# Pinning the opening of a fused attention and two-layer kernel, a score bank pair for each of its first four units, and weight words scaled on ACT from the sixth half on

## The chip, the core and the metric

The kernel runs as one program on one core of a Trainium2 chip. The metric is the device time of one execution in microseconds (us). The engines go by the profile's names: PE (TensorE, matmuls; PEld are its weight loads), DVE (VectorE), ACT (ScalarE), POOL (GpSimd, hardly used) and SP (SyncE, which issues nearly all DMAs). Each takes its own instructions strictly in the order in which the built program holds them and waits for others through semaphores.

## What is computed

The reference is local plus global attention, followed by two dense layers, all in float32:

```python
a_l = sm(s_l)                                   # window of 32 each way + 32 global keys
out_l = np.matmul(a_l, np.concatenate([v_g, v_l], axis=2))
out_g = np.matmul(sm(s_g), v_all)
x = concat([out_g, out_l]).transpose(0, 2, 1, 3).reshape(2176, 512)
h = x @ w_in;  g = np.maximum(h, 0.0) + alpha * np.minimum(h, 0.0);  x = g @ w_out      # first layer
h = x @ w_in2; g = h * np.clip(h + 3.0, 0.0, 6.0) / 6.0;             out = g @ w_out2   # second layer
```

There are 4 batches, 8 heads of 64, 512 local and 32 global positions; each layer goes 512 to 2048 to 512.

## The kernel before

**Attention.** The local attention is cut into 32 units (batch, half of the sequence, pair of heads), `local_units`, L177. A unit is 16 score matmuls into two PSUM banks (`s_ps`, L208), four row reductions with the mask on DVE (`p`, L226), four exponentials with their sums on ACT (L230), sums and reciprocals on DVE (`st`, `rs`, L232 and L234), four PE transposes (`pt_ps`, L241) and their copy to SBUF (`pt`, ACT, L243), 16 matmuls with the values (`o_ps`, L254) and a scaling on DVE (`xo`, L260). Units go in pairs that share the two score banks. Four units (0 to 3, the heads of the first 256 rows) make the first half of the first block of the first layer.

**Inputs of the first layer.** The `xo` tiles are transposed on PE (`xt_ps`, L426) and split into a high and a low float32r part: the high one by ACT (`xt`, L409), the low one by DVE (L410).

**Weights.** They arrive as 64-bit words, 512 columns (one *half*: one of 16 columns j of w_in or of w_out) per DMA (`raw`, L95). A half takes on ACT one scaling of the low words (`raw`, L110), then the scaling of the high words (`z`) on DVE (L113) or, from half `SCALED_ON_DVE` on, on ACT (L116), two DVE steps on bits (`z`, L121 and L123), a high part by ACT (`wt`, L132) and a low part by DVE (`wt`, L133). `z` has two buffers and `raw` five. From the half before `SCALED_ON_DVE` on, L169 begins the next half, too, before this one ends. The order of halves is in_0, in_1, out_0, in_2, out_1, in_3 and so on (L143); halves count from 0.

**First layer.** Block 0 goes in 20 steps. In the first four, `h_tile` (L453) makes 12 matmuls of 256 columns (`h_ps`, L459), one column j after the other, then `act` (L464) the PReLU: ACT `t` (L469), DVE `t` (L471), ACT `g` (L477), DVE `g` (L478). Two steps later the products with w_out follow (`y_ps`, L490). Four steps on, the second 256 rows (units 4 to 7) join. Between them attention steps and conversions are recorded (L1002 to L1008).

**What sets the order.** A scheduler places the recorded instructions by its own estimate of times; only what is wrapped in `here` (L100) stays at its place in the program. Before the first tile the conversions stand at attention steps 3, 4 and 5 (`CONVERT`, L44), and one more at step 0 of block 0 (L1002, L1003).

Of the kernel before, what the change touches and what calls it, by code (L numbers as in the profile page):

```python
# [21 lines left out]
HP = H // 2  # L22
# [20 lines left out]
SCALED_ON_DVE = 8  # L43
CONVERT = (3, 4, 5)  # L44
# [12 lines left out]
def fused_kernel(ctx, tc, qkE, vE, qgz, kN, vN, vgN, w1, w2, consts, out):  # L57
# [42 lines left out]
    here = tc.keep_in_program_order  # L100

# [17 lines left out]
    def end_float32(z, low, high):  # L119
        bits = z.bitcast(U32)  # L120
        nc.vector.scalar_tensor_tensor(out=bits, in0=bits, scalar=3, in1=low, op0=ALU.logical_shift_left,  # L121
                                       op1=ALU.bitwise_or)
        nc.vector.scalar_tensor_tensor(out=bits, in0=high, scalar=0x80000000, in1=bits, op0=ALU.bitwise_and,  # L123
                                       op1=ALU.bitwise_or)
        return z
# [4 lines left out]
    def split_w(begun, wt, m):  # L130
        z = end_float32(*begun)
        nc.scalar.copy(wt[:, m, 0, :], z)  # L132
        nc.vector.tensor_tensor(out=wt[:, m, 1, :], in0=z, in1=wt[:, m, 0, :].bitcast(F32), op=ALU.subtract)  # L133

    class Weights:
# [21 lines left out]

        def convert(self, halves):
            for _ in range(halves):
                k = self.next  # L160
                if k == 2 * NJ:
                    return
                self.fetch(EARLY)
                j, m = self.seq[k]
                if j not in self.wt:
                    self.wt[j] = wp.tile([128, 2, 2, 512], F32R, tag="w", name="wt", bufs=NJ)
                self.begin(k)
                if k + 1 >= SCALED_ON_DVE:
                    self.begin(k + 1)  # L169
                split_w(self.begun.pop(k), self.wt[j], m)  # L170
                self.fetch(k + EARLY + 1)
                self.next += 1
# [4 lines left out]
    def local_units(att):  # L177
        units = [(b, hf, hp) for b in range(B) for hf in range(2) for hp in range(HP)]
        q_t, k_t, v_t, p_t, rs_t, pt_t, v2 = {}, {}, {}, {}, {}, {}, {}
# [16 lines left out]
        def scores(*us):  # L196
            s = [bank("s0_ps"), bank("s1_ps")]
            for e, u in enumerate(us):
                b, hf, hp = units[u]
                q, k = q_t.pop(u), k_t.pop(u)  # L200
                for i in range(2):
                    for g in range(4):
                        at = 128 * i + W * g
                        o = W * (start_of(8 * hf + 4 * i + g) - 12 * hf)
                        to = 256 * e + 128 * i
                        for h in range(2):
                            rows = slice(64 * h, 64 * h + 64)
                            nc.tensor.matmul(s[h][W * g:W * g + W, to:to + 128], lhsT=q[rows, at:at + W],  # L208
                                             rhs=k[rows, o:o + 128], start=True, stop=True)
            for e, u in enumerate(us):  # L210
                softmax(u, [x[:, 256 * e:256 * e + 256] for x in s])

        def softmax(u, s):
# [8 lines left out]
            for i in range(2):  # L222
                m = 1 if (hf, i) == (0, 0) else 2 if (hf, i) == (1, 1) else 0
                for h in range(2):
                    n = 2 * i + h
                    nc.vector.tensor_tensor_reduce(  # L226
                        out=p[:, n, :], in0=s[h][:, 128 * i:128 * i + 128], in1=mask_sb[:, m, :],
                        op0=ALU.add, op1=ALU.min, scale=-0.125, scalar=-NEG, accum_out=st[:, 1, n:n + 1])
            for n in range(4):
                nc.scalar.activation(p[:, n, :], p[:, n, :], AF.Exp, bias=st[:, 1, n:n + 1], scale=-1.0,  # L230
                                     accum_out=st[:, 2, n:n + 1])
            nc.vector.tensor_scalar(out=st[:, 3, :], in0=st[:, 2, :], scalar1=1e-9, scalar2=None, op0=ALU.add)  # L232
            rs_t[u] = att.tile([128, 4], F32, tag="rs", name="rs", bufs=FIRST_UNITS)
            nc.vector.reciprocal(out=rs_t[u], in_=st[:, 3, :])  # L234
            p_t[u] = p

        def transposes(u):
            p = p_t.pop(u)
            t = bank("pt_ps")
            for n in range(4):  # L240
                nc.tensor.transpose(t[:, 128 * n:128 * n + 128], p[:, n, :], ident_sb)  # L241
            pt_t[u] = att.tile([128, 4, 128], F32, tag="pt", name="pt", bufs=2)
            nc.scalar.copy(pt_t[u], t.rearrange("p (n q) -> p n q", n=4))  # L243

        def values(*us):
            o = bank("o_ps")
            for e, u in enumerate(us):
                pt, v = pt_t.pop(u), v_t.pop(u)
                for i in range(2):
                    for h in range(2):  # L250
                        n = 2 * i + h
                        to = 256 * e + D * n
                        for g in range(4):
                            nc.tensor.matmul(o[W * g:W * g + W, to:to + D],  # L254
                                             lhsT=pt[:, n, W * g:W * g + W], rhs=v[:, 4 * i + g, h, :],
                                             start=True, stop=True)
            for e, u in enumerate(us):
                b, hf, hp = units[u]
                x = outs.tile([128, 2, 128], F32, tag="xo", name="xo", bufs=8)
                nc.vector.tensor_tensor(out=x.rearrange("p i (h d) -> p (i h) d", h=2),  # L260
                                        in0=o[:, 256 * e:256 * e + 256].rearrange("p (n d) -> p n d", n=4),
                                        in1=rs_t.pop(u)[:, :, None].to_broadcast([128, 4, D]), op=ALU.mult)
                xo[b, hf, hp] = x

# [13 lines left out]
        yield  # L278
        pairs = [(u, u + 1) for u in range(0, n, 2)]
        scores(*pairs[0])  # L280
        yield
        scores(*pairs[1])
        here(nc.vector.tensor_scalar(out=c1_sb, in0=alpha_sb, scalar1=-1.0, scalar2=1.0, op0=ALU.mult, op1=ALU.add))
        load(4)
# [8 lines left out]
        for u in pairs[1]:  # L293
            transposes(u)
        yield
        values(*pairs[1])
        yield
        for j in range(2, len(pairs) + 1):
            if j > 2:
                for u in pairs[j - 1]:  # L300
                    transposes(u)
# [3 lines left out]
            if j < len(pairs):  # L305
                scores(*pairs[j])
# [100 lines left out]

    def split_x(src, dst, n):
        nc.scalar.copy(dst[:, 0, :n], src)  # L409
        nc.vector.tensor_tensor(out=dst[:, 1, :n], in0=src, in1=dst[:, 0, :n].bitcast(F32), op=ALU.subtract)  # L410
# [4 lines left out]
    def x_transposed(pieces, each=1):  # L415
# [3 lines left out]
        for hp in range(HP):  # L419
# [3 lines left out]
            for piece in pieces:  # L423
                x = xo.pop(("g", hp) if piece == "g" else (*piece, hp))
                for i in range(1 if piece == "g" else 2):
                    nc.tensor.transpose(t[:, at:at + 128], x if piece == "g" else x[:, i, :], ident_sb)  # L426
# [26 lines left out]
    def h_tile(xt, wts, parts):  # L453
        ps = bank("h_ps")
        for a, b, j, at in parts:
            k = 0
            for c in range(NC):
                for wl, xl in ((0, 0), (1, 0), (0, 1)):
                    nc.tensor.matmul(ps[:, a:b], lhsT=wts[j][:, 0, wl, 128 * c:128 * c + 128],  # L459
                                     rhs=xt[c][:, xl, at:at + b - a], start=k == 0, stop=k == 3 * NC - 1)  # L460
# [3 lines left out]
    def act(layer, ps, parts):  # L464
# [3 lines left out]
        if layer == 0:  # L468
            nc.scalar.activation(t[:, a:b], ps[:, a:b], AF.Relu, scale=-1.0)  # L469
            for c, d, j, _ in parts:  # L470
                nc.vector.scalar_tensor_tensor(out=t[:, c:d], in0=t[:, c:d], scalar=c1_sb[:, j:j + 1],  # L471
                                               in1=ps[:, c:d], op0=ALU.mult, op1=ALU.add)
        else:
            nc.scalar.activation(t[:, a:b], ps[:, a:b], AF.Relu, bias=half_sb, scale=1.0 / 6.0)
            nc.vector.scalar_tensor_tensor(out=t[:, a:b], in0=t[:, a:b], scalar=1.0, in1=ps[:, a:b],
                                           op0=ALU.min, op1=ALU.mult)
        nc.scalar.copy(g[:, 0, a:b], t[:, a:b])  # L477
        nc.vector.tensor_tensor(out=g[:, 1, a:b], in0=t[:, a:b], in1=g[:, 0, a:b].bitcast(F32), op=ALU.subtract)  # L478
        return g

    def y_tiles(layer, y, g, wts, parts, lanes=False):
        for a, b, j, at in parts:
# [3 lines left out]
            for (wl, gl), c in steps:  # L486
                first = a == 0 and j == 0 and (wl, gl) == (0, 0)
                last = j == NJ - 1 and (wl, gl) == (0, 1) and (not lanes or b == 512)
                if layer == 0:
                    nc.tensor.matmul(y[c][:, at:at + b - a], lhsT=wts[j][:, 1, wl, 128 * c:128 * c + 128],  # L490
                                     rhs=g[:, gl, a:b], start=first, stop=last, skip_group_check=lanes)
                else:
                    nc.tensor.matmul(y[c], lhsT=g[:, gl, 128 * c:128 * c + 128], rhs=wts[j][:, 1, wl, :],
                                     start=first, stop=last)
# [485 lines left out]
    k = 0  # L980
    while not ready(blocks[0][:1]):
        attention_steps(1)
        k += 1
        if k in CONVERT:
            W1.convert(1)
    xt = x_tiles()
    x_split(x_transposed(blocks[0][:1]), xt, 0)
    spare["y"] = False
    for bi in range(len(blocks)):
# [5 lines left out]
        for s in range(end + LAG):  # L995
            if s < end:
                if bi == 0:
# [23 lines left out]
            if s >= LAG:  # L1021
                y_tiles(0, y, gs.pop(s - LAG), W1.wt, active(bi, s - LAG), bi == 0)
# [84 lines left out]
```

## Time and profile before

| what | us |
|---|---|
| median of three runs | 825.03 (823.32, 825.47, 825.03) |
| the profiled execution | 823.27 |
| its span, first to last instruction | 821.5 |
| PE busy | 809.2 (99%) |
| DVE busy | 596.6 (73%) |
| ACT busy | 423.3 (52%) |
| mean granted share of PE's clock | 0.993 |

The span is one execution of the program on the core; what lies outside of it, 1.8 us, is start and end. Shares are means over stages with different limits, so the opening has to be read by stretches.

### The profile page before, as it was taken

What the parts mean: (1) busy time and instruction counts of PE and PEld (TensorE: products, weight loads), DVE (VectorE), ACT (ScalarE), POOL (GpSimd) and SP (SyncE); (2) the same over time, 40 slices, a digit from 0 to 9 for tenths busy, and PEclk for the clock granted to TensorE, in tenths of its full rate; (3) what the DMA queues carried; (4) which work ended last, traced back from release to release, by engine and by line L of the source; (5) the groups of instructions that cost most, each with busy time, mean ns of one, the idle gap of its engine ahead of it and who ended that gap; (6) DMA issues with size and microseconds to landing.
All of it is one profiled execution on the core that took longest, in us unless ns stands there. A gap on an engine that the chain in (4) does not pass through costs nothing.

```text
span 821.5 us, 17564 instructions
## 1 busy us (share of the span) xinstructions
PE 809.2 (99%) x6980; PEld 714.1 (87%) x6980; DVE 596.6 (73%) x1247; ACT 423.3 (52%) x886; POOL 0.2 (0%) x4
## 2 busy tenths in 40 slices
PE   7999999999999999999999999999999999999997
PEld 4788888888888887888999988889999888899997
DVE  4998997477888776756878847778867576678443
ACT  5887996445656664544545524434553343333431
POOL 0000000000000000000000000000000000000000
PEclk8899999999999999999999999999999999999999
DMA  9985674347879767788495575576686656655663
GB/s 334 354 276 193 244 251 149 107 175 261 280 252 305 246 236 250 276 282 284 159 335 174 167 257 180 183 225 207 185 268 212 201 186 204 180 181 159 208 182 108
DMA packets 78002, 183.09 MB, mean 223 GB/s; under 512 B 6752, under 2 KB 28512, under 8 KB 77920
## 3 DMA queue, kind: packets, MB, share of 16 engines
q1 hardware_dynamic: 77728, 181.83, 66.9%
q8 instruction: 55, 0.90, 0.4%
q14 instruction: 27, 0.22, 0.1%
q10 hardware_dynamic: 192, 0.13, 0.1%
HBM read 139.47 MB, written 42.47 MB: 221 GB/s over the span
## 4 chain that ended last, share of the span: by engine, by line
PE 93%; DVE 2%; ACT 2%; DMA 1%; SPq 1%; issue 0%; DVEq 0%; ACTq 0%
PE y_ps L490 23%; PE h_ps L459 22%; PE o_ps L904 20%; PE k_ps L816 19%; PE s_ps L208 2%; PE o_ps L254 2%; PE yr_ps L789 1%; PE hr_ps L768 1%; DMA raw<-in_w 1%; PE pt_ps L241 1%; ACT p L230 1%; PE go_ps L391 1%; PE xt_ps L426 1%; PE gs_ps L346 1%; DVE z L121 1%
## 5 line engine op out<-in xcount | busy, mean ns | idle before, releaser
L490 PE MATMUL y_ps<-g,wt 128*128 128x512 f32 (+2 forms) x1008 | 205.4, 353 | 0.2 <-ACT g L477 0.2
L459 PE MATMUL h_ps<-xt,wt 128*128 128x512 f32 (+2 forms) x1008 | 203.2, 352 | 1.9 <-DVE xt L410 1.6
L459 PEld LDWEIGHTS h_ps<-xt,wt 128*128 128x128 f32 x1008 | 169.2, 190 | 24.0 <-DVE xt L410 2.0
L490 PEld LDWEIGHTS y_ps<-g,wt 128*128 128x128 f32 x1008 | 166.7, 189 | 22.2 <-issue 0.8
L904 PE MATMUL o_ps<-ws,gh 128*128 128x256 f32 x896 | 160.9, 283 | 0.1
L816 PE MATMUL k_ps<-bt,ws 128*128 128x512 f32 x672 | 157.2, 390 | 0.0
L816 PEld LDWEIGHTS k_ps<-bt,ws 128*128 128x128 f32 x672 | 124.6, 188 | 24.9
L904 PEld LDWEIGHTS o_ps<-ws,gh 128*128 128x128 f32 x896 | 138.8, 192 | 0.6 <-issue 0.3
L904 PE MATMUL o_ps<-ws,gl 128*128 128x256 f32 x448 | 124.2, 283 | 0.0
L830 DVE TENSOR_TENSOR gl<-far,gh 128x1024 fp32r<-128x1024 f32 x56 | 68.5, 1223 | 42.3 <-ACT gh L829 42.3
L829 ACT CAST gh<-far 128x1024 fp32r<-128x1024 f32 x56 | 58.7, 1048 | 74.4 <-PE o_ps L904 70.6
L904 PEld LDWEIGHTS o_ps<-ws,gl 128*128 128x128 f32 x448 | 84.9, 192 | 0.0
L471 DVE SCALAR_TENSOR_TENSOR t<-t,c_sb,h_ps 128x512 f32<-128x512 f32 (+2 forms) x84 | 53.0, 641 | 30.0 <-ACT t L469 29.6
L750 ACT ACTIVATE t<-far,half_sb 128x512 f32<-128x512 f32 x48 | 34.8, 724 | 77.1 <-DVE far L746 77.1
L469 ACT ACTIVATE t<-h_ps 128x512 f32<-128x512 f32 (+2 forms) x76 | 41.5, 550 | 51.0 <-PE h_ps L459 49.0
L478 DVE TENSOR_TENSOR g<-t,g 128x512 fp32r<-128x512 f32 (+2 forms) x76 | 48.0, 632 | 20.8 <-ACT g L477 18.4
L477 ACT CAST g<-t 128x512 fp32r<-128x512 f32 (+2 forms) x76 | 43.8, 576 | 34.7 <-DVE t L471 33.4
L230 ACT ACTIVATE p<-p,st 128x128 f32<-128x128 f32 x128 | 49.7, 389 | 11.6 <-DVE st L226 11.6
L121 DVE SCALAR_TENSOR_TENSOR z<-z,raw 128x512 uint32<-128x512 uint32 x64 | 43.6, 689 | 9.1 <-ACT z L116 4.6
L110 ACT ACTIVATE raw<-raw,quarter_sb 128x512 uint32<-128x512 uint32 x64 | 49.3, 772 | 1.6 <-DMA raw<-in_w 1.6
L123 DVE SCALAR_TENSOR_TENSOR z<-raw,z 128x512 uint32<-128x512 uint32 x64 | 43.4, 688 | 0.6
L751 DVE SCALAR_TENSOR_TENSOR far<-t,far 128x512 f32<-128x512 f32 x48 | 33.1, 689 | 11.8 <-ACT t L750 11.8
(102 smaller groups left out, 786.5 us busy)
## 6 DMA issues: line engine op xcount, KB each, us to landing
raw<-in_w SPq DMA_DIRECT2D x64, 512.0 KB, 5.4
ws<-wo SPq DMA_DIRECT2D x60, 512.0 KB, 3.8
ws<-wi SPq DMA_DIRECT2D x56, 512.0 KB, 4.4
v_t<-in_vE SPq DMA_DIRECT2D x32, 512.0 KB, 6.9
qk_t<-in_qkE SPq DMA_DIRECT2D x32, 368.0 KB, 5.1
wi<-raw SPq DMA_DIRECT2D x16, 512.0 KB, 3.3
wi<-parts SPq DMA_DIRECT2D x16, 512.0 KB, 4.5
wo<-raw SPq DMA_DIRECT2D x16, 512.0 KB, 2.9
```

The lines of the kernel that those rows point to most:

```text
L110: here(nc.scalar.activation(low, low, AF.Relu, bias=quarter_sb, scale=0.9 * 2.0 ** -29))
L121: nc.vector.scalar_tensor_tensor(out=bits, in0=bits, scalar=3, in1=low, op0=ALU.logical_shift_left, op1=ALU.bitwise_or)
L230: nc.scalar.activation(p[:, n, :], p[:, n, :], AF.Exp, bias=st[:, 1, n:n + 1], scale=-1.0, accum_out=st[:, 2, n:n + 1])
L459: nc.tensor.matmul(ps[:, a:b], lhsT=wts[j][:, 0, wl, 128 * c:128 * c + 128], rhs=xt[c][:, xl, at:at + b - a], start=k == 0, stop=k == 3 * ...
L471: nc.vector.scalar_tensor_tensor(out=t[:, c:d], in0=t[:, c:d], scalar=c1_sb[:, j:j + 1], in1=ps[:, c:d], op0=ALU.mult, op1=ALU.add)
L477: nc.scalar.copy(g[:, 0, a:b], t[:, a:b])
L478: nc.vector.tensor_tensor(out=g[:, 1, a:b], in0=t[:, a:b], in1=g[:, 0, a:b].bitcast(F32), op=ALU.subtract)
L490: nc.tensor.matmul(y[c][:, at:at + b - a], lhsT=wts[j][:, 1, wl, 128 * c:128 * c + 128], rhs=g[:, gl, a:b], start=first, stop=last, skip_g ...
L816: nc.tensor.matmul(bank, lhsT=wt[:, wl, 128 * c:128 * c + 128], rhs=bt[x][:, c, xl, 0:w], start=first and k == 0, stop=k == 5, skip_group_ ...
L829: nc.scalar.copy(hi, src)
L830: nc.vector.tensor_tensor(out=lo, in0=src, in1=hi.bitcast(F32), op=ALU.subtract)
L904: mm = nc.tensor.matmul(bank, lhsT=part[:, jp, 128 * c:128 * c + 128], rhs=wo[:, jp, 256 * wl:256 * wl + 256], start=opens, stop=k == NP / ...
```

## The change

`SCALED_ON_DVE` goes from 8 to 5, so the high words of halves 5, 6 and 7 are scaled by ACT, and the beginning of the next half is recorded ahead from half 4 on. A function `keep` pins everything up to the first PReLU step into program order. Units 0 to 3 are recorded one by one, each with two score banks of its own. The copies of the transposed probabilities of units 0, 1 and 2 go from ACT to DVE. The first half's conversion and the beginning of the second are woven between the transposes of x; no other conversion stands ahead of the first tile, and step 0 records none ahead of it (`if s`). The two DMAs of the values of units 4 and 5 come ahead of that of half 3.

```diff
-SCALED_ON_DVE = 8
-CONVERT = (3, 4, 5)
+SCALED_ON_DVE = 5
...
     here = tc.keep_in_program_order
+    pinned = {"on": True}
+
+    def keep(x):
+        return here(x) if pinned["on"] else x
...
+        for u in range(FIRST_UNITS):
+            s = [bank("s0_ps"), bank("s1_ps")]
+            scores(u, s, 0)
+            maxima(u, s, 0)
+            exponentials(u)
+        t = {}
+        for u in range(2):
+            t[u] = transposes(u)
+            sums(u)
+            transposed(u, t[u], nc.vector.tensor_copy)
+        keep(nc.vector.tensor_scalar(out=c1_sb, in0=alpha_sb, scalar1=-1.0, scalar2=1.0, op0=ALU.mult, op1=ALU.add))
+        t[2] = transposes(2)
+        values(0)
+        sums(2)
+        transposed(2, t[2], nc.vector.tensor_copy)
+        t[3] = transposes(3)
+        sums(3)
+        values(1)
+        yield
         load(5)
-        yield
-        for u in pairs[0]:
-            transposes(u)
-        yield
-        values(*pairs[0])
+        transposed(3, t[3], nc.scalar.copy)
+        yield
         load_v(4)
         load_v(5)
...
-    k = 0
-    while not ready(blocks[0][:1]):
-        attention_steps(1)
-        k += 1
-        if k in CONVERT:
-            W1.convert(1)
     xt = x_tiles()
-    x_split(x_transposed(blocks[0][:1]), xt, 0)
+    half = W1.one()
...
+    attention_steps(1)
+    t0 = turn(0)
+    high_x(t0, xt[0], 256)
+    attention_steps(1)
+    t1 = turn(1)
+    high_x(t1, xt[1], 256)
+    next(half)
+    low_x(t0, xt[0], 256)
+    low_x(t1, xt[1], 256)
+    next(half)
+    attention_steps(1)
+    next(half)
+    t2 = turn(2)
...
+    for _ in half:
+        pass
+    half = W1.one()
+    next(half)
+    next(half)
...
-                    W1.convert(W1.needed(converted(s)) - W1.next)
-                    W1.convert(min(1, W1.needed(converted(s) + AHEAD) - W1.next))
+                    if s:
+                        W1.convert(W1.needed(converted(s)) - W1.next)
+                    if s:
+                        W1.convert(min(1, W1.needed(converted(s) + AHEAD) - W1.next))
                 parts = active(bi, s)
-                gs[s] = act(0, h_tile(xt, W1.wt, parts), parts)
+                gs[s] = act(h_tile(xt, W1.wt, parts), parts, half)
+                pinned["on"] = False
```

`next(half)` runs a conversion up to its next `yield`: first its beginning (L110, L113 of before), then the bit steps, then the two parts. The rest of the diff splits helpers so that they can be recorded apart, and drops a branch that nothing calls.

**ACT around the first tiles.** `wt` is a half's high part, `raw` the scaling of low words, `p` an exponential, `xt` the high part of x, `t` and `g` the PReLU. Before, from the first `wt` (half 0) on:

```order
L132 CAST wt<-z 128x512
L409 CAST xt<-xt_ps 128x256
L132 CAST wt<-z 128x512
L110 ACTIVATE raw<-raw,quarter_sb 128x512
L409 CAST xt<-xt_ps 128x256
L110 ACTIVATE raw<-raw,quarter_sb 128x512
L132 CAST wt<-z 128x512 x2
L230 ACTIVATE p,st<-p,st 128x128 x3
```

In the changed kernel, from the third `wt` (half 2) to the fourth (half 3):

```order
L136 CAST wt<-z 128x512
L113 ACTIVATE raw<-raw,quarter_sb 128x512
L242 ACTIVATE p,st<-p,st 128x128
L515 ACTIVATE t<-h_ps 128x256
L242 ACTIVATE p,st<-p,st 128x128 x5
L113 ACTIVATE raw<-raw,quarter_sb 128x512 x2
L521 CAST g<-t 128x256
L113 ACTIVATE raw<-raw,quarter_sb 128x512
L269 COPY pt<-pt_ps 128x512
L136 CAST wt<-z 128x512
```

Before, half 3 follows half 2 at once and both stand ahead of all exponentials of the second four units; now six exponentials, three scalings of low words and three other rows stand between the two.

**PE around the third tile.** `h_ps` x12 is one column of the first layer, `pt_ps` and `s_ps` belong to units 4 to 7. Before, from the rest of the second column on:

```order
L459 MATMUL h_ps<-xt,wt 128x256 x13
L241 MATMUL pt_ps<-consts_sb,p 128x128 x5
L459 MATMUL h_ps<-xt,wt 128x256 x12
L241 MATMUL pt_ps<-consts_sb,p 128x128 x3
L490 MATMUL y_ps<-g,wt 128x256 x8
```

In the changed kernel, from the second column on:

```order
L505 MATMUL h_ps<-xt,wt 128x256 x12
L264 MATMUL pt_ps<-consts_sb,p 128x128 x2
L534 MATMUL y_ps<-g,wt 128x256 x4
L264 MATMUL pt_ps<-consts_sb,p 128x128
L534 MATMUL y_ps<-g,wt 128x256 x8
L264 MATMUL pt_ps<-consts_sb,p 128x128 x5
L505 MATMUL h_ps<-xt,wt 128x256
L216 MATMUL s_ps<-qk_t 32x128 x17
L505 MATMUL h_ps<-xt,wt 128x256 x11
```

The third column (the one that needs half 3) has moved behind the first 12 products with w_out, and the scores of units 6 and 7 stand behind its first matmul. From the 24 `h_ps` of the third and fourth column of the second 256 rows on, PE's rows run alike in both programs.

## Rows read from the trace of the kernel before

**Rows 1.** Busy time of each engine by stretches (us of the span).
```profile
core 0: us, PE busy (x) PEld busy (x) DVE busy (x) ACT busy (x) POOL busy (x), PEclk, DMA share, GB/s
...
30.00:40.00 10.00, 9.13 (x180) 7.24 (x183) 9.40 (x36) 9.43 (x28) 0.00 (x0) 1.00 0.89 300
40.00:50.00 10.00, 8.29 (x164) 6.93 (x156) 9.42 (x39) 9.61 (x34) 0.00 (x0) 1.00 0.90 310
60.00:800.00 740.00, 740.00 (x6033) 656.33 (x6015) 542.59 (x1062) 373.66 (x741) 0.00 (x0) 1.00 0.67 218
```

**Rows 2.** Chain that ended last, about 50 us: start, length, what.
```profile
49.50 0.34 DVE xt L410
49.89 1.57 PE h_ps L459 x11
```

**Rows 3.** Timeline of PE: start, length, line, count, [idle before, releaser].
```profile
16.97 1.08 PE L254 MATMUL o_ps<-v_t,pt 128*32 128x64 f32 x32
...
23.22 2.45 PE L459 MATMUL h_ps<-xt,wt 128*128 128x256 f32 x10
...
29.02 1.69 PE L459 MATMUL h_ps<-xt,wt 128*128 128x256 f32 x12
...
54.56 3.04 PE L459 MATMUL h_ps<-xt,wt 128*128 128x256 f32 x24
```

**Rows 4.** Timeline of ACT, 6 to 49 us.
```profile
6.65 0.40 ACT L230 ACTIVATE p<-p,st 128x128 f32<-128x128 f32 x1 [4.64 <-DVE st L226]
...
29.50 0.39 ACT L230 ACTIVATE p<-p,st 128x128 f32<-128x128 f32 x1
...
29.89 0.77 ACT L110 ACTIVATE raw<-raw,quarter_sb 128x512 uint32<-128x512 uint32 x1
30.55 0.36 ACT L469 ACTIVATE t<-h_ps 128x256 f32<-128x256 f32 x1
30.81 0.39 ACT L477 CAST g<-t 128x256 fp32r<-128x256 f32 x1
31.11 1.05 ACT L243 COPY pt<-pt_ps 128x512 f32<-128x512 f32 x2
...
43.53 1.14 ACT L132 CAST wt<-z 128x512 fp32r<-128x512 f32 x2
...
48.11 0.67 ACT L116 ACTIVATE z<-raw 128x512 f32<-128x512 f32 x1
```

**Rows 5.** Timeline of DVE, 13 to 49 us.
```profile
14.26 0.42 DVE L113 TENSOR_SCALAR z<-raw 128x512 f32<-128x512 f32 x1
...
24.27 0.68 DVE L121 SCALAR_TENSOR_TENSOR z<-z,raw 128x512 uint32<-128x512 uint32 x1
24.99 0.69 DVE L123 SCALAR_TENSOR_TENSOR z<-raw,z 128x512 uint32<-128x512 uint32 x1
25.60 0.68 DVE L133 TENSOR_TENSOR wt<-z,wt 128x512 fp32r<-128x512 f32 x1
26.20 0.28 DVE L226 CUSTOM_DVE_ANT_0 p<-s_ps,consts_sb 128x128 f32<-128x128 f32 x1
...
27.68 0.69 DVE L133 TENSOR_TENSOR wt<-z,wt 128x512 fp32r<-128x512 f32 x1
...
38.29 0.74 DVE L260 TENSOR_TENSOR xo<-o_ps,rs 128x256 f32<-128x256 f32 x2
...
48.29 0.39 DVE L410 TENSOR_TENSOR xt<-xt_ps,xt 128x256 fp32r<-128x256 f32 x1
```

**Rows 6.** The one DVE copy out of a PSUM bank, all its runs.
```profile
L1039 DVE COPY ev<-y_ps x10: 425/681/692, 141.8 to 479.7; 128x512 f32<-128x512 f32 x6, 128x256 f32<-128x256 f32 x2, 128x384 f32<-128x384 f32 x2
```

**Rows 7.** The same stretches view for PE with the granted clock.
```profile
4.99:15.23 10.24, 7.64 (x220) 1.00 1.00 358
15.23:25.47 10.24, 8.55 (x135) 0.50 1.03 407
25.47:35.71 10.24, 9.76 (x189) 1.00 0.94 356
```

More of the change, by code (lines that the diff above doesn't have):

```diff
@@ L120, in end_float32 @@
         bits = z.bitcast(U32)
[L121 to L124, printed above, removed]
+        keep(nc.vector.scalar_tensor_tensor(out=bits, in0=bits, scalar=3, in1=low, op0=ALU.logical_shift_left,
+                                            op1=ALU.bitwise_or))
+        keep(nc.vector.scalar_tensor_tensor(out=bits, in0=high, scalar=0x80000000, in1=bits, op0=ALU.bitwise_and,
+                                            op1=ALU.bitwise_or))
         return z
@@ L131, in split_w @@
         z = end_float32(*begun)
-        nc.scalar.copy(wt[:, m, 0, :], z)
-        nc.vector.tensor_tensor(out=wt[:, m, 1, :], in0=z, in1=wt[:, m, 0, :].bitcast(F32), op=ALU.subtract)
+        yield
+        keep(nc.scalar.copy(wt[:, m, 0, :], z))
+        keep(nc.vector.tensor_tensor(out=wt[:, m, 1, :], in0=z, in1=wt[:, m, 0, :].bitcast(F32), op=ALU.subtract))
+        yield
     class Weights:
@@ L156, in begin, with one @@
                 self.begun[k] = begin_float32(self.raw.pop(k), k < SCALED_ON_DVE)
+        def one(self):
+            k = self.next
+            self.fetch(EARLY)
+            j, m = self.seq[k]
+            if j not in self.wt:
+                self.wt[j] = wp.tile([128, 2, 2, 512], F32R, tag="w", name="wt", bufs=NJ)
+            self.begin(k)
+            yield
+            if k + 1 >= SCALED_ON_DVE:
+                self.begin(k + 1)
+            yield from split_w(self.begun.pop(k), self.wt[j], m)
+            self.fetch(k + EARLY + 1)
+            self.next += 1
         def convert(self, halves):
             for _ in range(halves):
-                k = self.next
-                if k == 2 * NJ:
+                if self.next == 2 * NJ:
                     return
[L163 to L172, printed above, removed]
+                for _ in self.one():
+                    pass
     xo = {}
@@ L194, in load_v, with scores, maxima @@
             nc.sync.dma_start(out=v_t[u], in_=vE[b, hp, :, 8 * hf:8 * hf + 8])
[L196 to L213, printed above, removed]
+        def scores(u, s, to):
+            b, hf, hp = units[u]
+            q, k = q_t.pop(u), k_t.pop(u)
+            for i in range(2):
+                for g in range(4):
+                    at = 128 * i + W * g
+                    o = W * (start_of(8 * hf + 4 * i + g) - 12 * hf)
+                    for h in range(2):
+                        rows = slice(64 * h, 64 * h + 64)
+                        mm = nc.tensor.matmul(s[h][W * g:W * g + W, to + 128 * i:to + 128 * i + 128],
+                                              lhsT=q[rows, at:at + W], rhs=k[rows, o:o + 128], start=True, stop=True)
+                        if u < FIRST_UNITS or u == FIRST_UNITS and i == g == h == 0:
+                            here(mm)
+        def maxima(u, s, to):
             b, hf, hp = units[u]
@@ L278, in local_units @@
         yield
+        load(4)
         pairs = [(u, u + 1) for u in range(0, n, 2)]
-        scores(*pairs[0])
+        for u in range(FIRST_UNITS):
+            s = [bank("s0_ps"), bank("s1_ps")]
+            scores(u, s, 0)
+            maxima(u, s, 0)
+            exponentials(u)
+        t = {}
+        for u in range(2):
+            t[u] = transposes(u)
+            sums(u)
+            transposed(u, t[u], nc.vector.tensor_copy)
[7 more added lines that the diff above has]
+        values(1)
         yield
-        scores(*pairs[1])
-        here(nc.vector.tensor_scalar(out=c1_sb, in0=alpha_sb, scalar1=-1.0, scalar2=1.0, op0=ALU.mult, op1=ALU.add))
-        load(4)
         load(5)
+        transposed(3, t[3], nc.scalar.copy)
         yield
-        for u in pairs[0]:
-            transposes(u)
-        yield
-        values(*pairs[0])
         load_v(4)
         load_v(5)
-        for u in pairs[1]:
-            transposes(u)
+        values(2)
         yield
-        values(*pairs[1])
+        values(3)
         yield
@@ L406, in fused_kernel, with high_x, low_x, x_transposed @@
     rows = out.rearrange("(b s) d -> b s d", s=S)
+    def high_x(src, dst, n):
+        keep(nc.scalar.copy(dst[:, 0, :n], src))
+    def low_x(src, dst, n):
+        keep(nc.vector.tensor_tensor(out=dst[:, 1, :n], in0=src, in1=dst[:, 0, :n].bitcast(F32), op=ALU.subtract))
     def split_x(src, dst, n):
-        nc.scalar.copy(dst[:, 0, :n], src)
-        nc.vector.tensor_tensor(out=dst[:, 1, :n], in0=src, in1=dst[:, 0, :n].bitcast(F32), op=ALU.subtract)
+        high_x(src, dst, n)
+        low_x(src, dst, n)
     def x_tiles():
         return [work.tile([128, 2, 512], F32R, tag="xt", name="xt", bufs=HP) for _ in range(HP)]
-    def x_transposed(pieces, each=1):
+    def x_transposed(pieces, each=1, pairs=range(HP)):
         n = sum(128 if x == "g" else 256 for x in pieces)
         parts = []
-        for hp in range(HP):
+        for hp in pairs:
             if hp % each == 0:
@@ L458, in h_tile, with act @@
                 for wl, xl in ((0, 0), (1, 0), (0, 1)):
-                    nc.tensor.matmul(ps[:, a:b], lhsT=wts[j][:, 0, wl, 128 * c:128 * c + 128],
-                                     rhs=xt[c][:, xl, at:at + b - a], start=k == 0, stop=k == 3 * NC - 1)
+                    mm = nc.tensor.matmul(ps[:, a:b], lhsT=wts[j][:, 0, wl, 128 * c:128 * c + 128],
+                                          rhs=xt[c][:, xl, at:at + b - a], start=k == 0, stop=k == 3 * NC - 1)
+                    keep(mm)
                     k += 1
         return ps
-    def act(layer, ps, parts):
+    def act(ps, parts, between=()):
         t = work.tile([128, 512], F32, tag="t", name="t", bufs=TB)
@@ L467, in act, with y_tiles @@
         a, b = parts[0][0], parts[-1][1]
[L468 to L478, printed above, removed]
+        keep(nc.scalar.activation(t[:, a:b], ps[:, a:b], AF.Relu, scale=-1.0))
+        for c, d, j, _ in parts:
+            keep(nc.vector.scalar_tensor_tensor(out=t[:, c:d], in0=t[:, c:d], scalar=c1_sb[:, j:j + 1],
+                                                in1=ps[:, c:d], op0=ALU.mult, op1=ALU.add))
+        for _ in between:
+            pass
+        keep(nc.scalar.copy(g[:, 0, a:b], t[:, a:b]))
+        keep(nc.vector.tensor_tensor(out=g[:, 1, a:b], in0=t[:, a:b], in1=g[:, 0, a:b].bitcast(F32),
+                                     op=ALU.subtract))
         return g
-    def y_tiles(layer, y, g, wts, parts, lanes=False):
+    def y_tiles(y, g, wts, parts, lanes=False):
         for a, b, j, at in parts:
@@ L488, in y_tiles @@
                 last = j == NJ - 1 and (wl, gl) == (0, 1) and (not lanes or b == 512)
[L489 to L494, printed above, removed]
+                nc.tensor.matmul(y[c][:, at:at + b - a], lhsT=wts[j][:, 1, wl, 128 * c:128 * c + 128],
+                                 rhs=g[:, gl, a:b], start=first, stop=last, skip_group_check=lanes)
     half_sb = const.tile([128, 1], F32, name="half_sb")
```

64 lines of the change are left out of this document (43 added, 21 removed).

## The prediction

> **What bounds the kernel now.** I read the stretches first: from 60 to 800 us PE is busy for 740.00 of 740 us, while DVE and ACT have a fifth to a half of it free [rows 1]. Nothing that DVE or ACT gain or lose there shows. From 30 to 50 it is the other way round: DVE is busy for 9.40 and 9.42 of ten, ACT for 9.43 and 9.61, and PE has holes [rows 1]. The chain of waits says when the roles change: its last DVE piece, the low part of x, begins at 49.50, and from 49.89 it is PE alone [rows 2]. So I need one number: how far the change moves the moment at which PE reaches its solid part. As a mark I take the 24 `h_ps` matmuls at 54.56 [rows 3]. From there PE's rows are the same in both orders, and ahead of it stand the same 72 `h_ps` and 48 `y_ps` matmuls; whatever moves the mark moves the end by as much.
>
> **What it adds, removes and moves.**
>
> *Scaling of halves 5, 6 and 7.* DVE loses 3 x 0.34 (the step from 14.26 to 14.60) [rows 5] = 1.0 us, ACT gains 3 x 0.67 [rows 4] = 2.0 us. Neither is covered: both engines are full until 50.
>
> *Copies of `pt`.* ACT loses 3 x 0.52 [rows 4]. DVE has not made this copy; its copy of the same size out of a bank took 0.68 at the median [rows 6], so I take steps of 0.60, with ACT's 0.52 and 0.80 as bounds. They come at 10 to 13 us.
>
> *DMAs.* The values of units 4 and 5 pass the words of half 3. At the 0.4 MB per us of the full queue (407 GB/s in 15 to 25 us) [rows 7], two transfers of 0.52 MB make these 2.6 us later. I put their landing at 24 to 25; DVE asks for half 3 at 28. They cost nothing; with that cover gone, up to 2.6.
>
> *Conversions.* This is the large edit. Before, half 3 stood ahead of the exponentials of the second four units, and its low part began on DVE at 27.68 [rows 5]; the third column of the first layer, which needs it, started at 29.02 [rows 3]. Now it stands behind six exponentials and three scalings for later halves. I work the queues forward in their new order, each step as long as its row, each wait for what the program waits for. The same working of the order before puts the third column at 29.0 and the mark at 54.3 (trace 29.02 and 54.56).
>
> 1. *To the first tile.* One unit's scores now suffice for the first exponential, which I put at 5.65 instead of 6.65 [rows 4]. Sixteen in a row at 0.39 end at 11.9. Transposes, the values of unit 1 and two transposes of x take until 13.0 (an estimate from the same rows). ACT: two `xt` and a `pt` copy, then the low words of half 0 (0.66), to 14.8. DVE: `z` 0.72, `z` 0.61 [rows 5], `xo` 0.4, to 16.6. PE at the lower clock: two transposes, then 16 value matmuls in 1.08 [rows 3], to 18.3; `xo` and two more transposes: **19.2**. Before, only one matmul ran ahead of 23.22 [rows 3]. So the front is indeed earlier.
> 2. *To half 2.* 12 matmuls at 0.245 (2.45 for ten) [rows 3] end at 22.2, with their latency 22.4. ACT `t` and `wt` of half 1, then on DVE `wt` 0.60, `g` 0.39, scaling 0.34, `z` 0.60, two maxima 0.42, `z` 0.69 [rows 5]: the high part of half 2 starts on ACT at **26.4**.
> 3. *ACT to half 3.* `wt` 0.57, then `raw` 0.66, `p` 0.39, `t` 0.26, five `p` 1.95, two `raw` 1.32, `g` 0.30, `raw` 0.66, `pt` 0.52 [rows 4]. That is 6.6, so 33.0; with `wt` itself, DVE's low part and with it the third column start at **33.6**. DVE had half 3's bits ready near 30.4. Against 27.68 and 29.02 this is +5.9 and +4.6.
> 4. *From there to the split at 48.29* [rows 5]. Between the two, DVE's rows sum to 17.95 us in the new order and to 17.99 in the old one. The new one waits 1.0 more, mostly for ACT's `z`: 55.1 against 48.2.
> 5. *From the split to the mark.* Two of the halves that follow are already converted, so this is shorter by 0.6: 5.5 against 6.1.
>
> Sum: 5.9 + 1.0 - 0.6 = 6.3, or 60.6 against 54.3 at the mark; against the traced 54.56 it is 6.0. I take **+6.2**.
>
> *A second count.* Ahead of the split at 48.29 DVE now holds 6 more `z` rows (3.6 us), 2 more `wt` (1.2) and 3 copies (1.8), and 3 scalings (1.0) and three small rows (0.3) fewer: +5.3. The copies fall into a part in which DVE waits anyway, so at least +3.5 of it counts. Conversions have been pulled ahead of a point that PE waits for, out of a part in which they were free. Bounds: +3.5 from below; from above +7.4, with copies at 0.80 (0.6 on leg 1) and another 0.6 of waiting. PE at full clock in leg 1 would take off 0.2 to 1.2.
>
> *PE's clock.* It has one stretch at the lower level, 15.23 to 25.47, granted 0.50 (1.2 of 2.4 GHz), right after an opening in which PE was busy for 7.64 of 10.24 us [rows 7]. The new order makes PE wait 3.2 us ahead of the third column (30.5 to 33.6) and 3.1 ahead of the fourth (37.2 to 40.4), so a second such stretch is possible. While PE waits for others it costs nothing. On the solid part it costs half its length, 5.1 us. The Trainium skill ("TensorE: Matmul & The Clock Gate", "HAM oscillation — how this bites in real kernels") tells of a matmul kernel that was put back to the lower clock at every wait for data; by that rule the change would end 5 us later still. The trace agrees as to the opening, but holds no wait followed by solid work, so I keep this as a rival.
>
> **Time.** The sum goes against the profiled execution's own 823.27: 829.5. The three runs shown have their mean at 824.75 and their median at 825.03, 1.5 and 1.8 above it. So I forecast **831.0** for the median.
>
> **Rivals.**
>
> *The opening wins (faster).* By the working above the second column ends about 1 us earlier than before. If the pinned order also removed the holes that PE shows from 30 to 50, 0.87 + 1.71 [rows 1], the gain would be 3.6: 821.4. It decides at 29.0: half 3's low part must start on DVE before that. For it speaks the earlier front; against it that ACT's rows between halves 2 and 3 stand there in any case, and sum to 6.6. Chance 0.07.
>
> *Nothing changes.* Both engines catch up before 49.9, because DVE's and ACT's rows in the opening are the same work in another order: 825. It needs 5 us of idle time on both; they had 1.2 and 1.0 in 20 us [rows 1]. It is also the outcome if the order does less than it says. Chance 0.10.
>
> *A second stretch at the lower clock on the solid part*, as above: 831.0 + 5.1 = 836.1. For it the waits of 3 us, against it that PE has work for most of the time between 40 and 57. Chance 0.12.
>
> **How the numbers follow.** My forecast has 0.71; its bounds, +3.5 and +7.4 over the runs' mean of 824.75, give 828.3 and 832.2, and the runs' own spread some 1.5 more at either end. The range of 8 in 10 reaches from 827.0 to 836.0: it leaves out the faster case, most of the one without change, and a tail of the clock case. A measurement of this kernel can tell some 0.3%, 2.5 us. Faster 0.07, same 0.10, slower 0.71 + 0.12 = 0.83.
>
> **What would show it.** Right: the first tile's 12 `h_ps` in one run from 19 to 22 us; ACT rows without a hole from 26.5 to 33; the third column at 33 to 34 and the split of the second rows at 54 to 56; PE solid from about 57 and the 24 `h_ps` at 60 to 61.5. Wrong: the third column before 30, or the split before 50; then the legs on ACT are mistaken. A granted clock of 0.50 after 56 us would be the clock rival.

## The result, and the profile of the changed kernel

The changed kernel takes 830.69 us (median of six runs, 829.84 to 832.37), the kernel before 825.23 beside it (six runs): a ratio of 1.0070, with a 95% interval of 1.0054 to 1.0086. It is slower by 5.5 us; the forecast was 831.0. A second measurement gave 830.64, ratio 1.0067 (1.0052 to 1.0083). There are two profiled executions of it, of 832.37 us (span 830.6) and of 829.54 (span 827.7), to be set against the 823.27 (span 821.5) of before. The second, nearer to the median, is called `again` here. Both 823.27 and 829.54 are among the fastest runs of their kernels (823.28 to 827.45 in the runs of before beside the experiments, 829.44 to 832.49 in those of `again`), so these two can be compared.

| moment, us | before | worked for the change | first profile | `again` |
|---|---|---|---|---|
| first `h_ps` tile begins | 20.08 | 19.2 | 20.19 | 19.23 |
| ACT begins the high part of half 2 | – | 26.4 | 27.23 | 26.26 |
| ACT begins the high part of half 3 | – | 33.0 | 33.67 | 32.70 |
| third column begins | 29.02 | 33.6 | 34.35 | 33.38 |
| DVE splits the second 256 rows of x | 48.29 | 55.1 | 55.97 | 54.92 |
| the mark: 24 `h_ps` in a row | 54.56 | 60.6 | 63.33 | 60.74 |
| end of the span | 821.5 | – | 830.6 | 827.7 |

Busy time by stretches in the first profile, in the columns of [rows 1]:

```profile
30.00:40.00 10.00, 7.00 (x148) 5.39 (x146) 8.08 (x17) 8.46 (x20) 0.00 (x0) 0.83 0.69 241
40.00:50.00 10.00, 6.82 (x108) 5.28 (x96) 9.46 (x34) 8.97 (x29) 0.00 (x0) 1.00 0.93 320
60.00:800.00 740.00, 739.95 (x6025) 655.44 (x6024) 542.69 (x1066) 376.48 (x750) 0.00 (x0) 1.00 0.66 216
```

From 60 to 800 us PE is as solid as before. From 30 to 50 PE has lost 3.60 us of work, and from 30 to 40 DVE and ACT, which were full before, now have idle time: they wait for each other. PE in `again` (timeline, as in [rows 3]):

```profile
19.23 2.81 PE L505 MATMUL h_ps<-xt,wt 128*128 128x256 f32 x12
...
33.38 0.58 PE L505 MATMUL h_ps<-xt,wt 128*128 128x256 f32 x1 [2.90 <-ACT wt L136]
...
55.39 0.62 PE L505 MATMUL h_ps<-xt,wt 128*128 128x256 f32 x3
56.49 0.51 PE L505 MATMUL h_ps<-xt,wt 128*128 128x256 f32 x2 [0.48 <-ACT xt L449]
57.28 2.29 PE L505 MATMUL h_ps<-xt,wt 128*128 128x256 f32 x17 [0.29 <-DVE xt L452]
...
60.74 3.13 PE L505 MATMUL h_ps<-xt,wt 128*128 128x256 f32 x24
```

The chain of waits of `again` hands over to PE at the same kind of place as in [rows 2], 7.4 us later:

```profile
56.90 0.34 DVE xt L452
57.24 0.04 issue
57.28 2.29 PE h_ps L505 x17
```

The first tile begins 0.85 us earlier than before and, its 12 matmuls now in one run, ends at 22.04; before, its last matmul stood in the row that begins at 25.96. So some 4 us were won here, and more than that is lost by the third column. The third column then waits 2.90 us for the high part of half 3. Where that comes from shows on ACT (timeline of `again`; left out are the short reads of the exponentials' sums, four more exponentials and one more scaling of low words):

```profile
26.26 0.60 ACT L136 CAST wt<-z 128x512 fp32r<-128x512 f32 x1
26.77 0.76 ACT L113 ACTIVATE raw<-raw,quarter_sb 128x512 uint32<-128x512 uint32 x1
27.43 0.39 ACT L242 ACTIVATE p<-p,st 128x128 f32<-128x128 f32 x1
...
27.81 0.36 ACT L515 ACTIVATE t<-h_ps 128x256 f32<-128x256 f32 x1
28.08 0.39 ACT L242 ACTIVATE p<-p,st 128x128 f32<-128x128 f32 x1
...
30.00 1.39 ACT L113 ACTIVATE raw<-raw,quarter_sb 128x512 uint32<-128x512 uint32 x2
31.29 0.40 ACT L521 CAST g<-t 128x256 fp32r<-128x256 f32 x1
...
32.24 0.57 ACT L269 COPY pt<-pt_ps 128x512 f32<-128x512 f32 x1
32.70 0.62 ACT L136 CAST wt<-z 128x512 fp32r<-128x512 f32 x1
```

ACT has no hole from one high part to the next: from the start of the one to the start of the other it is 6.44 us, where the working had 6.6.

**Where DVE's time went.** The best account is of DVE ahead of PE's first matmul on the second 256 rows (48.74 before, 55.39 in `again`), one stretch from the start, first before, then `again`:

```profile
0.00:48.74 48.74, 41.00 (x717) 30.65 (x717) 36.39 (x157) 37.03 (x123) 0.20 (x4) 0.89 0.93 334
```

```profile
0.00:55.39 55.39, 42.99 (x728) 32.56 (x728) 43.06 (x163) 39.86 (x125) 0.20 (x4) 0.91 0.91 330
```

DVE is busy for 36.39 us before and for 43.06 now, and idle for 12.35 and for 12.33. So in this count the whole +6.65 is DVE work that now stands ahead of the point. Busy and idle time of one engine add up to the moment in any case: the count sorts a delay, and what causes it has to come from the experiments. Its rows, grouped, again before and then `again` (count, then busy time, mean ns, idle time ahead):

```profile
L121 DVE SCALAR_TENSOR_TENSOR z<-z,raw 128x512 uint32<-128x512 uint32 x8 | 5.4, 681 | 0.2
L123 DVE SCALAR_TENSOR_TENSOR z<-raw,z 128x512 uint32<-128x512 uint32 x8 | 5.4, 680 | 0.0
L133 DVE TENSOR_TENSOR wt<-z,wt 128x512 fp32r<-128x512 f32 x8 | 5.4, 678 | 0.0
L113 DVE TENSOR_SCALAR z<-raw 128x512 f32<-128x512 f32 x8 | 3.3, 413 | 1.1 <-DMA raw<-in_w 1.1
...
L232 DVE TENSOR_SCALAR st<-st 128x4 f32<-128x4 f32 x10 | 1.7, 165 | 4.1 <-ACT p L230 4.1
```

```profile
L126 DVE SCALAR_TENSOR_TENSOR z<-raw,z 128x512 uint32<-128x512 uint32 x11 | 7.6, 689 | 0.1
L124 DVE SCALAR_TENSOR_TENSOR z<-z,raw 128x512 uint32<-128x512 uint32 x11 | 7.6, 688 | 1.8 <-ACT z L119 1.2 <-ACT raw L113 0.3
L137 DVE TENSOR_TENSOR wt<-z,wt 128x512 fp32r<-128x512 f32 x10 | 6.9, 688 | 2.3 <-ACT wt L136 2.2
...
L452 DVE TENSOR_TENSOR xt<-xt_ps,xt 128x256 fp32r<-128x256 f32 x5 | 2.1, 421 | 1.0 <-ACT xt L449 1.0
L116 DVE TENSOR_SCALAR z<-raw 128x512 f32<-128x512 f32 x5 | 2.1, 414 | 0.0
L269 DVE COPY pt<-pt_ps 128x512 f32<-128x512 f32 x3 | 2.0, 658 | 0.0
```

Six more bit steps (+4.4), two more low parts (+1.5), three copies (+2.0), three scalings fewer (-1.2); these are sums of the rows' own lengths, which overlap with the row behind by up to 0.1 us each, so they are not exact. The waits kept their sum and changed their kind: 4.1 us for exponentials and 1.1 for words have gone (the rows of `st` and of `z<-raw` before), 3.4 for ACT's `wt` and `z` and 1.0 for its `xt` have come, the rest in small pieces.

From that point to the mark it is 5.35 in `again` and was 5.82, so the mark moves by 6.18 and the span by 6.2. In all twelve profiles of this study the span ends between 766.8 and 768.2 us behind the mark: the mark carries the end.

### The profile page after: what moved, and what is told of

The parts are those of the page before. It is cut to its first block, busy times and chain, and to the rows that moved or that the text cites. A ratio compares the mean times of both kernels' runs of the same rounds, so it can differ in the third digit from the quotient of the medians.

```text
span 830.6 us, 17570 instructions
## 1 busy us (share of the span) xinstructions
PE 809.6 (97%) x6980; PEld 714.6 (86%) x6980; DVE 598.8 (72%) x1247; ACT 424.0 (51%) x886; POOL 0.2 (0%) x4
## 4 chain that ended last, share of the span: by engine, by line
PE 93%; ACT 3%; DVE 2%; DMA 1%; issue 0%; SPq 0%; DVEq 0%; ACTq 0%
PE y_ps L534 22%; PE h_ps L505 22%; PE o_ps L946 19%; PE k_ps L858 18%; PE o_ps L280 2%; PE s_ps L216 1%; PE yr_ps L831 1%; PE hr_ps L810 1%; DMA raw<-in_w 1%; PE pt_ps L264 1%; ACT p L242 1%; PE xt_ps L472 1%; PE gs_ps L386 1%; PE go_ps L431 1%; DVE z L124 1%; ACT raw L113 1%
## 5 line engine op out<-in xcount | busy, mean ns | idle before, releaser
L113 ACT ACTIVATE raw<-raw,quarter_sb 128x512 uint32<-128x512 uint32 x64 | 49.5, 775 | 0.4 <-DMA raw<-in_w 0.4
```

What stands on the lines that cost most here:

```text
L113: here(nc.scalar.activation(low, low, AF.Relu, bias=quarter_sb, scale=0.9 * 2.0 ** -29))
```

## The experiments

The table gives for each kernel the moments of its profile, and DVE's busy and idle time ahead of PE's first matmul on the second rows ("split"). Times are medians; the ratio is to the kernel before, run beside it, with its 95% interval. The moments are those of one execution each, and not of a median one: the profile of before (823.27) lies 1.5 to 2 us below the medians in its row, so a mark set against 54.56 says that much too much for a kernel whose profile lies at its median. The first loads alone move the front: the first exponential starts at 6.65 in before and at 7.91 in `c34`, which issues the same DMAs in the same order.

| kernel | third column | split | DVE busy / idle ahead | mark | time | ratio |
|---|---|---|---|---|---|---|
| before | 29.02 | 48.74 | 36.39 / 12.35 | 54.56 | 824.8 to 825.2 | 1 |
| the change, `again` | 33.38 | 55.39 | 43.06 / 12.33 | 60.74 | 830.64 | 1.0067 (1.0052 to 1.0083) |
| `c34` | 34.47 | 56.23 | 41.00 / 15.23 | 60.23 | 829.22 | 1.0052 (1.0037 to 1.0067) |
| `c3` | 33.35 | 54.34 | 42.23 / 12.11 | 58.35 | 827.53 | 1.0035 (1.0022 to 1.0049) |
| `s5` | 29.33 | 50.15 | 36.91 / 13.24 | 56.94 | 826.17 | 1.0014 (1.0004 to 1.0024) |
| `after_dve8` | 34.06 | 56.32 | 44.38 / 11.94 | 60.85 | 829.24 | 1.0051 (1.0038 to 1.0063) |
| `copies_act` | 35.78 | 54.49 | 37.40 / 17.09 | 59.90 | 828.66 | 1.0048 (1.0029 to 1.0067) |
| `unpinned` | 34.63 | 53.21 | 38.71 / 14.50 | 58.62 | 829.65 | 1.0051 (1.0036 to 1.0066) |
| `undone` | 30.70 | 50.89 | 38.22 / 12.67 | 56.17 | 825.94 | 1.0015 (1.0004 to 1.0026) |
| `words_first` | 29.14 | 48.87 | 36.37 / 12.50 | 54.69 | 824.28 | 0.9990 (0.9981 to 0.9999) |
| `words_first_dve6` | 28.94 | 48.58 | 36.34 / 12.24 | 53.87 | 824.18 | 0.9988 (0.9979 to 0.9996) |

**The change once more (`again`).** No edit.

> The changed kernel once more, unaltered. Its one profile had the mark (the 24 h_ps) at 63.33 and a half-speed stretch of PE from 58.85 to 62.26. Order theory: in another execution the landings and the half-speed stretches differ by a microsecond or three, but the third column starts at 33 to 35, the split comes at 55 to 57 and the mark at 60 to 63; time 829.5 to 831.5. Clock rival (the loss is mostly half-speed stretches behind waits): without one on the solid part the mark would be near 57 and the time near 827.

Measured: the mark at 60.74 without a half-speed stretch on the solid part, and 830.64. The loss is there without the clock's help, so the clock rival falls as the main cause.

**One conversion fewer ahead of the first tile, alone (`c34`).**

```diff
-CONVERT = (3, 4, 5)
+CONVERT = (3, 4)
```

> The kernel before with one conversion fewer ahead of its first tile (half 2 and not half 3 the last), and nothing else: no pinning, no pt copies on DVE, DVE scales up to half 7. Order theory (conversions behind exponentials): third column at 33 to 34, split near 53, mark 4.6 us later than in the kernel before, 829.0 to 831.0 in time. Rivals (scaling on ACT, copies on DVE, pinning cost the time): none of these is here, so 825 to 826.

Measured: 829.22, +4.4, with none of the other edits in it. PE's timeline shows the same wait as in the change:

```profile
34.47 0.38 PE L459 MATMUL h_ps<-xt,wt 128*128 128x256 f32 x1 [2.29 <-ACT wt L132]
```

This is the result that carries most: one half that slips behind the exponentials costs as much alone as three quarters of the change. Here 4.61 of the 7.49 us at the split are more DVE work ahead, 2.88 are more waiting; 1.3 of the waiting is for the first scores (6.7 us where before had 5.4), which this edit does not touch. The time came as expected and the way there did not: the split was to come near 53 and came at 55.78 on DVE and 56.23 on PE, and what lies between split and mark got shorter, 4.00 us where it was 5.82.

**Halves 1, 2 and 3 whole, ahead of the first PReLU (`c3`).**

```diff
-    half = W1.one()
-    next(half)
-    next(half)
+    W1.convert(3)
+    half = ()
```

> The changed kernel with half 3 converted whole (and half 2 before it) ahead of the first PReLU, in place of the partial conversion; all else as in the change. Order theory: third column near 32 in place of 33.6, mark 2.9 us earlier than in the changed kernel, 827.0 to 829.0; not all comes back, since the conversions of halves 2 and 3 now delay the first PReLU. Rivals: conversions are not what costs, so 830 to 831, or above if the first tiles wait longer.

Measured: 827.53, 3.1 less, as worked, but not by the way that I gave. The third column was to come at 32 and came at 33.35, since the scheduler left half 3's high part behind eight exponentials (ACT, 32.67). What got shorter lies behind it: 1.05 at the split, 1.34 from there to the mark. So conversions recorded ahead help, and a late third column alone is not what sets the end. (In this profile the first tile begins at 20.32, 1.1 us later than in `again`; so the gain is not from the front.)

**Scaling of halves 5 to 7 (`s5`, `after_dve8`).** In the kernel before, `SCALED_ON_DVE = 5`; in the changed kernel, `SCALED_ON_DVE = 8`.

> The kernel before with halves 5, 6 and 7 scaled on ACT (SCALED_ON_DVE at 5) and nothing else. Order theory: ACT and DVE take this in the order of before with +0.7 us at the mark, 825.2 to 826.8. Scaling rival (3 x 0.67 us more on a full ACT, and the next half begun too early, are the main cost): 828 or more.

> The changed kernel with halves 5, 6 and 7 scaled on DVE again (SCALED_ON_DVE at 8) and nothing else. Order theory: mark 1.2 us earlier than in the changed kernel, third column at 33, 829.0 to 830.3. Scaling rival (the scaling on ACT is the main part of the loss): 827 or less.

Measured: +1.4 in the one, -1.4 in the other (its profile is of its slowest execution, 830.87 us, so the table's mark is no measure of it). The mark of `s5` was to move by 0.7 and stands 2.4 later. Some 1.5 of that is PE's clock, granted at 0.50 from about 50.3 to 53.7 and thus on the solid part: 18 `h_ps` took 3.93 us, where 17 took 2.29 in `again`. Without it the mark would stand some 0.9 later (an estimate from these rows).

```profile
50.15 3.93 PE L459 MATMUL h_ps<-xt,wt 128*128 128x256 f32 x18 [1.82 <-DVE xt L410]
```

The scaling rival asked for 3 or more and falls as the main cause; the edit has a price of about 1.4 in either surrounding, though the interval of `after_dve8` overlaps that of the change.

**Copies of `pt` back on ACT, and nothing pinned (`copies_act`, `unpinned`).**

```diff
-            transposed(u, t[u], nc.vector.tensor_copy)
+            transposed(u, t[u], nc.scalar.copy)
...
-        transposed(2, t[2], nc.vector.tensor_copy)
+        transposed(2, t[2], nc.scalar.copy)
```

```diff
-    pinned = {"on": True}
+    pinned = {"on": False}
```

> The changed kernel with the copies of pt of units 0, 1 and 2 on ACT again and nothing else. It puts the late third column against the rows ahead of the split: working the queues forward, the scheduler places what follows in another order, so that the third column comes 1.1 us later than in the changed kernel (34.7) and the split of x all the same 3.3 earlier (51.8), the mark 3.2 earlier: 827.0 to 828.5. If the third column's start sets all that follows: 831 to 832. If only the copies themselves counted: 0.2 to 1.0 less than the changed kernel, 829.7 to 830.5.

> The changed kernel with nothing pinned by keep (its switch off from the start); copies of pt still on DVE for units 0, 1 and 2. Left to itself the scheduler puts the rows behind the second column on ACT and DVE in the same order as in copies_act. If copies_act gained by that order and not by its copies: split near that of copies_act (54.5), mark near 59.9 and 827.5 to 829.0. If the copies on DVE are themselves the price, the gain is not here: 830 to 831. Pinning as such the whole loss: 825 to 826.

Measured: 828.66 and 829.65, 0.2 and 0.7 above what the order theory expected, both with intervals that overlap the change's, so neither gain is clear of the noise. The working for `copies_act` was off by more than its time: the mark was to come 3.2 earlier and came 0.8 earlier. The profiles still show one thing. In both the third column comes later than in the change (35.78 and 34.63), and the split comes earlier (54.49 and 53.21). So the third column's start alone does not set what follows. DVE has 5.7 and 4.3 us less work ahead of the split, but gets only 0.9 and 2.2 of it, because it waits more. In `copies_act` most of that is for PE's products with the values (in `unpinned` 1.3 us are):

```profile
L286 DVE TENSOR_TENSOR xo<-o_ps,rs 128x256 f32<-128x256 f32 x8 | 3.3, 420 | 4.5 <-PE o_ps L280 4.5
```

Which of the two edits is worth how much stays open: both lead the scheduler to the same later order, and the times of either scatter (827.07 to 831.79 and 827.16 to 830.98; the profile of `unpinned` belongs to its 827.16). What sets one execution of them apart from the next was not found.

**Four edits undone at once (`undone`).** Both diffs above, `SCALED_ON_DVE = 8`, and `W1.convert(2)` in the place of `W1.convert(3)` in `c3`.

> The changed kernel with four of its edits undone at once: not pinned, copies on ACT, halves 5 to 7 scaled on DVE, halves 1 and 2 converted whole ahead of the first PReLU; units one by one with banks of their own and the order of DMAs stay as in the change. Order theory: third column at 31 to 32.5, mark 4.3 us earlier than in the changed kernel, 825.8 to 827.8. If the four gains add up (3.1 of c3, 1.4 of after_dve8, 2.0 of copies_act): 824 to 825. If units one by one or the DMAs are a price of their own: 828 or more.

Measured: 825.94, in the range of the order theory; the third column, at 30.70, came a little before it. The single gains (3.1, 1.4, 2.0) don't add up: 6.5 would lie below the kernel before, 4.7 was had. The comparison is rough, since `c3` converts one half more ahead and two of the three gains are not clear of the noise. The profile suggests that they are in part one gain: DVE has 4.8 us less work ahead of the split than in `again`, while its idle time is no less (12.67 against 12.33). What is left, 1.1 us (interval 0.3 to 2.1), is the net of all that still differs from before, among it units one by one, banks of their own, the order of the DMAs and a later half 3. None of these was run alone.

**Words ahead of values (`words_first`, `words_first_dve6`).** In the kernel before, the first words are fetched ahead of the values of units 0 and 1, the next ahead of those of units 2 and 3; in the second kernel also `SCALED_ON_DVE = 6`.

```diff
         load(3)
+        yield
         load_v(0)
         load_v(1)
         yield
         load_v(2)
         load_v(3)
-        yield
```

> The kernel before with the DMA of the words of the first half issued ahead of those of the values of units 0 and 1, and the next words ahead of units 2 and 3; nothing else. Order theory (the opening's conversions set when PE gets solid): first words and first tile 1.2 us earlier, mark about 1.2 earlier: 823.0 to 824.2. Rival (the opening's lead is lost behind DVE's and ACT's later rows, or the values now come late): 824.5 or more.

> As words_first, with halves 6 and 7 scaled on ACT (SCALED_ON_DVE at 6). Working the queues forward: mark 0.5 earlier again, 822.5 to 823.8. Scaling rival: later than words_first by 1 to 2 us.

Measured: 824.28 and 824.18, below both kernels, by 0.10% and 0.12%. That is less than worked for either, and the profile of `words_first` does not show the worked way: the waits for words (1.1 us on DVE) have gone, but ACT reaches the first words at 14.18, behind its exponentials, where it was 13.78, and the mark is at 54.69 and not earlier. The exponentials themselves start at 7.83 in this profile and at 6.65 in that of before. Whether the edit delays them or only this execution did is open: they start at 7.91 in `c34` without the edit. In `words_first_dve6` the mark is at 53.87. So `words_first_dve6` has the lowest median here, 0.04 to 0.21% below the kernel before; between it and `words_first` no difference is shown.

## Why the prediction was right, and where not

*The bound and the mark*: right. PE solid from the mark on, the distance from there to the end constant to 1.4 us over twelve profiles. The forecast of 831.0 is the sum in the profiled execution (829.5; `again` took 829.54) and 1.5 for the median. The medians moved by 5.5 and 5.9 and not by 6.2, a difference within their intervals.

*Leg 1, first tile at 19.2*: 19.23 in `again`, 20.19 in the first profile, in which DVE waited 1.26 us for the first words (the row at 14.26 of [rows 5] has no such wait). That `again` meets it to 0.03 is in part luck: its first exponential came at 6.15 (worked 5.65) and the `xo` worked to end at 16.6 ended at 17.41, but PE was not at the lower clock yet, so that the value matmuls ahead of the tile took 0.65 where 1.08 was worked. The wait in the first profile:

```profile
14.91 0.43 DVE L116 TENSOR_SCALAR z<-raw 128x512 f32<-128x512 f32 x1 [1.26 <-DMA raw<-in_w]
```

*Legs 2 and 3*: right to 0.3 us in `again`. ACT between the halves was 6.44 against 6.6.

*Leg 4, to the split at 55.1*: 54.92. *Leg 5 and the sum*: mark at 60.74 against 60.6, span +6.2 against +6.2.

*The three terms of the sum*: each came out. Half 3's low part on DVE begins at 33.36 in `again`, where it began at 27.68: +5.7 for 5.9. From there to the split at 54.92 DVE is busy for 18.80 us where it was 18.78, and idle for 2.76 where it was 1.83: +0.9 for 1.0. From there to the mark it is 0.45 less, for 0.6. Together 6.2.

*Half 3 as what decides*: here the reasoning claimed too much. For the faster case it named one condition, half 3's low part on DVE before 29.0. In this kernel half 3, the split and the mark go together, but `c3` gained 3.1 us with that row at 33.33 and an unchanged third column, and `copies_act` reached the split earlier with a later column. What stands behind half 3 on DVE, and how long DVE waits there, counts as well.

*The second count*: it named the right rows (six more bit steps, two low parts, three copies, three scalings fewer) and undersized them, +6.67 in the trace against +5.3. The copies are not why. They were worked in steps of 0.60, from the start of one row to that of the next, and such a step is 0.57 in `again`, a little less (the 0.66 of the grouped row is a copy's whole length, which overlaps with the row behind):

```profile
10.38 0.66 DVE L269 COPY pt<-pt_ps 128x512 f32<-128x512 f32 x1
10.95 0.16 DVE L247 TENSOR_SCALAR st<-st 128x4 f32<-128x4 f32 x1
```

The bit steps and low parts are part of it. They count with 0.60 only where the next row starts into their end; with a wait behind them, as behind half 3's low part, they count whole, with 0.69. Where the rest of the 1.4 us comes from was not traced. "At least +3.5 of it counts" held as a bound, but its reason was not the right one. The copies did come where DVE waited before, and still the idle time in total stayed at 12.3, since other waits came behind them. That the two idle times agree to 0.02 us is, as far as the runs show, chance: in `c34` and `copies_act` they are 15.23 and 17.09.

*DMAs at nothing*: right. In `again` DVE waits for no words at half 3.

*The clock rival*: its mechanism occurred, and at under a third of its price. In `again` PE's clock is granted at 0.50 from 33.06, 0.3 us before the wait of 2.90 us ends, to 39.70. That stretch is off the solid part, and from 33 to 40 us no row of DVE or ACT is shown waiting for PE. It goes with the late third column: all seven profiles in which that starts after 33 us have a stretch at 0.50 that begins between 31 and 36.2 us, and the five in which it starts before 31 have none between 27 and 50. What sets it off is not shown. It need not be free in all of them: in `copies_act` DVE waits 1.36 us for scores at 38.26, inside of it. In the first profile one lay on the solid part, after 56 us, the sign that the prediction named for this rival:

```profile
34.95:38.37 3.42, 3.42 (x45) 2.89 (x22) 2.40 (x5) 2.61 (x5) 0.00 (x0) 0.50 0.74 248
38.37:58.85 20.48, 15.83 (x296) 12.58 (x296) 18.24 (x68) 16.94 (x55) 0.00 (x0) 1.00 0.88 296
58.85:62.26 3.41, 3.41 (x18) 3.41 (x18) 0.10 (x1) 0.00 (x0) 0.00 (x0) 0.50 0.28 108
```

There the 17 `h_ps` that took 2.29 us in `again` took 3.61:

```profile
58.34 3.61 PE L505 MATMUL h_ps<-xt,wt 128*128 128x256 f32 x17 [0.29 <-DVE xt L452]
```

That is +1.3, and from the split to the mark 6.88 against 5.35. I had priced it at 5.1, half of the 10.24 us of the only such stretch that before showed; here one lasts 3.41, and half of that is 1.7. Together with the late words (1.1 at the split) it makes up the 2.6 us between the two profiles' marks. The Trainium skill ("TensorE: Matmul & The Clock Gate", "HAM oscillation — how this bites in real kernels") tells of a matmul kernel that went back to the lower clock at every wait for data. The traces agree with that for the wait at 33 us. The fall at 58.85 us is of another kind: in the 20.48 us before it PE was busy for 15.83 and had no wait longer than 1.1, and the same rows with the same small waits (0.48 and 0.29) ran at full clock in `again`. What set it off was not found.

## What to carry to other kernels

Where a stretch bound by DVE and ACT is followed by one bound by PE, find the moment at which PE becomes solid, and count two things ahead of it: the busy time of the engines that gate it, and their idle time. An edit that starts the first tile earlier can lose more than it gained if it lets a conversion slip behind a batch of other rows on a full engine, or pulls work ahead of that moment that was free behind it. Single gains found by undoing edits need not add up where a scheduler reorders all that follows each of them.

## What the runs showed that was not expected

PE's half-speed stretches move from execution to execution of the same program: in the changed kernel 17.89 to 21.30, 34.95 to 38.37 and 58.85 to 62.26 in one, and about 19.3 to 22.8 and 33.06 to 39.70 in the other; `words_first_dve6` has one at about 7.6 to 11 us and none behind it. On PE's solid part there was one in two of the twelve profiles (the first of the change and `s5`); of about 3.4 us each, they cost 1.3 to 1.5 us. And DVE's idle time ahead of the split was the same to 0.02 us in the two kernels, although what it waited for was not the same.
